# Another hand-written order of units, with other engines for the casts and copies, in a kernel of windowed attention and a maxout layer

## The chip, the core and the metric

The kernel runs on one core of a Trainium2 chip. The metric is device time in microseconds (us), and the median of three runs before the change is 180.03 us (179.86 to 180.07). Engines are called as in the profile: PE is TensorE (PEld its weight loads), DVE VectorE, ACT ScalarE, POOL GpSimd, SP the engine that issues nearly all transfers. A letter q behind an engine means its queue of instructions.

## What is computed

Attention over 4 batches x 8 heads, 768 positions, head size 64, and then a layer in which three products are reduced by a maximum. The mask keeps the first 8 positions (global) and the last 96 before each position (local).

```python
scores = scale * np.matmul(q, k.transpose(0, 1, 3, 2))
keep = is_global | is_local          # pos < 8, or 0 <= rel < 96
bias = -slopes[:, None, None] * dist[None, :, :]
scores = np.where(keep, scores + bias, -1000000000.0)
a = softmax(scores)
x = (a @ v).transpose(0, 2, 1, 3).reshape(3072, 512)
h = np.maximum(np.maximum(x @ w1, x @ w2), x @ w3)   # 512 -> 768
out = h @ w_out                                      # 768 -> 512
```

Inputs and output are float32; the matmuls run in bf16.

## The kernel before

The 3072 positions are 24 tiles of 128, six to a batch. The string `SCHEDULE` is a list of units, and each unit's letter picks a function (the dictionary `units` at the end). Every engine gets its instructions in the order of this list, and so does the SP queue its transfers; nothing reorders them. Numbers behind the letter are the tile or part, and the last one often picks the engine (`copies`: 0 ACT, 1 DVE, 2 POOL).

- Loads, all on SP: `l` (`load_part`, L151, q or k of a group of tiles), `L` (`load`, q and k of one tile), `v` (`load_v`), `w` (`load_w`, w1 to w3: 256 columns for g = 0, 512 for g = 1), `o` (`load_wo`). `raw` has five buffers, `rawv` six.
- Casts to bf16: `c` (`cast_part`), `C` (`cast`: `C T.0` q and k, `C T.1` v; a last number of 3 gives q to DVE and k to POOL), `W`, `Q` (weights).
- Transposes of q and k: `x` (parts; 4 and above split the eviction between ACT and DVE) and `X` (tiles). `X T.4` is a DMA transpose on SP (L250), the others are PE transposes with an eviction.
- Scores `S T.g.how` (`u_S`, L268) for heads 4g to 4g+3, with the exp on ACT (L288). With how = 1 the bias is added by two further matmuls; with 0 the unit `M` multiplies P by a mask on DVE. `K` and `B` make the masks and biases once. `G` (`put_kg`) copies the global keys over the first rows of a tile's k after its own scores, and the next tile's scores need them there. `V` (`put_vg`) does this for v.
- `A T` (`u_A`, L311): P times v on PE, then the normalisation on DVE (L331, L332) into `xb`. `T` (`u_XT`): transposes xb into `xT`, by PE or, with 4, by DMA (L340).
- `F c.f.j` (`u_F1`, L355): one of the 18 products of a chunk (chunks hold 4, 2, 2, 4, 4, 4 and 4 tiles, so matmuls are 512 or 256 wide), evicted by ACT for j = 0 and by a maximum on DVE for j = 1 and 2. `O c.tt.how` (`u_F2`): the second product of one tile, its copy and its store. `E` is the last chunk's second product, with its last store on ACT's queue.
- `D i.n` (`u_D`, L432): n matmuls of zeros that nothing reads.

In PSUM there are three buffers `psH` (F, O, some transposes, D), one `psT` (transposes), and two `sp` tags that scores and `A` share.

Of the kernel before, what the change touches and what calls it, by code (L numbers as in the profile page):

```python
# [22 lines left out]


SCHEDULE = """
    K0 K1 K2 K3 K4 K5 l1.0 l1.1 D0.3 c0.0.2 B0.1 B1.1 B2.1 B3.0 K6 B4.1 B5.1 c0.1.1 c1.0.2 x0.0.4 B6.1
    B7.1 x0.1.4 S0.0.1 v0 l2.0 l2.1 K7 S0.1.1 G0.0 S1.0.1 S1.1.0 x1.0.3 c1.1.2 M0.0 M0.1 M1.0 v1 x1.1.4
    C0.1.2 v2 A0.1 G1.2 S2.0.1 M1.1 c2.0.2 x2.0.1 C1.1.1 S2.1.0 G2.2 S3.0.1 M2.0 M2.1 C2.1.1 T0.1 S3.1.1
    M3.0 M3.1 c2.1.2 v3 A1.0 C3.1.0 w0.0 V1.2 x2.1.2 w1.0 A2.1 V2.2 A3.0 T1.0 T2.1 T3.1 W1.0.1 W0.0.0
    G3.2 S4.0.0 S4.1.0 F0.0.0 F0.1.0 M4.0 F0.2.0 F0.3.0 G4.1 S5.0.0 M4.1 S5.1.0 w0.1 W0.1.1 w0.2 W0.2.2  # L30
    V3.2 F0.0.1 F0.1.1 F0.0.2 F0.1.2 v4 C4.1.0 A4.0 V4.2 w1.1 W1.1.2 W2.0.0 F0.4.0 F0.5.0 M5.0 M5.1 w1.2
    W1.2.2 v5 W2.1.0 T4.0 F0.2.1 F0.3.1 l3.0 l3.2 F0.4.1 l3.1 c3.0.2 c3.2.2 F0.5.1 o2 C5.1.0 A5.1 l3.3
    F0.2.2 Q2.2 F0.3.2 W2.2.0 o0 T5.0 F0.4.2 o1 F0.5.2 x3.0.0 F1.0.0 F1.1.0 c3.1.1 F1.2.0 x3.2.0 Q0.2
    F1.0.1 F1.1.1 F1.2.1 l4.0 l4.1 c3.3.0 F1.0.2 F1.1.2 F1.2.2 x3.1.2 x3.3.1 F1.3.0 F1.4.0 Q1.2 F1.3.1
    S6.0.0 S6.1.0 v6 v7 v8 G6.0 F1.3.2 F1.5.0 v9 c4.0.1 F1.4.1 S7.0.0 S7.1.0 G7.2 v10 M6.0 M6.1 M7.0
    M7.1 O0.0.0 F1.4.2 c4.1.1 C6.1.2 C7.1.2 L12 F1.5.1 S8.0.0 S8.1.0 x4.0.0 O0.1.0 A6.0 x4.1.2 A7.1 V7.2
    F1.5.2 v11 T6.0 O0.2.0 T7.1 G8.2 C8.1.2 S9.0.0 S9.1.0 G9.1 v12 v13 O0.3.0 F2.0.0 F2.1.0 S10.0.0 M8.0
    M8.1 M9.0 M9.1 S10.1.0 C9.1.2 L13 L14 F2.0.1 F2.1.1 F2.0.2 A8.0 C12.0.1 F2.1.2 G10.2 O1.0.0 V8.2
    A9.1 X12.1 M10.0 M10.1 C10.1.0 C11.1.0 F2.2.0 S11.0.0 S11.1.0 M11.0 M11.1 L15 F2.3.0 F2.4.0 O1.1.0
    V9.2 A10.1 F2.2.1 V10.2 T8.0 F2.3.1 F2.5.0 T9.0 A11.1 F2.4.1 T10.0 F2.2.2 F2.3.2 T11.1 F2.4.2  # L40
    S12.0.0 S12.1.0 F2.5.1 C13.0.2 C14.0.2 C15.0.1 X13.4 F3.0.0 F3.1.0 F3.0.1 G12.1 C12.1.0 F3.2.0
    F3.1.1 F3.2.1 S13.0.0 S13.1.0 F2.5.2 v14 C13.1.0 C14.1.2 M12.0 M12.1 F3.0.2 F3.1.2 X14.4 F3.2.2
    X15.4 G13.2 M13.0 M13.1 S14.0.0 S14.1.0 F3.3.0 F3.4.0 F3.5.0 M14.0 M14.1 G14.1 A12.0 A13.1 F3.3.1
    F3.4.1 F3.5.1 S15.0.0 M15.0 S15.1.0 G15.0 v15 V13.2 L16 L17 v16 T12.4 v17 M15.1 O2.0.0 C15.1.0 A14.0
    V14.2 F3.3.2 F3.4.2 T13.4 F3.5.2 C16.1.0 C16.0.2 X16.3 T14.4 C17.0.2 A15.1 X17.4 O2.1.0 S16.0.0
    S16.1.0 G16.1 L18 V15.2 L19 T15.1 M16.0 O3.0.0 M16.1 F4.0.0 F4.1.0 F4.0.1 F4.1.1 C18.0.2 L20 C19.0.2
    A16.1 F4.2.0 F4.3.0 S17.0.0 S17.1.0 F4.2.1 F4.0.2 F4.3.1 v18 M17.0 v19 M17.1 X18.3 X19.4 C20.0.0
    V16.2 F4.1.2 C17.1.2 O3.1.1 A17.1 F4.2.2 F4.3.2 S18.0.0 M18.0 S18.1.0 M18.1 F4.4.0 T16.4 T17.4
    F4.4.1 C18.1.2 C19.1.1 F4.4.2 X20.4 G18.1 S19.0.0 S19.1.0 F4.5.0 L21 M19.0 M19.1 v20 F4.5.1 A18.0
    T18.4 F4.5.2 A19.1 T19.4 V19.1 C21.0.1 X21.4 G19.1 L22 C22.0.2 L23 X22.4 O3.2.1 O3.3.0 O4.0.1  # L50
    S20.0.0 S20.1.0 M20.0 G20.0 O4.1.0 F5.0.0 F5.1.0 F5.2.0 S21.0.0 S21.1.0 G21.2 F5.0.1 F5.1.1 M20.1
    M21.0 F5.3.0 F5.0.2 F5.1.2 F5.2.1 F5.2.2 v21 C20.1.1 C21.1.2 F5.4.0 S22.0.0 M21.1 S22.1.0 C23.0.0
    F5.3.1 M22.0 M22.1 F5.5.0 F5.3.2 A20.0 V20.2 G22.2 v22 F5.4.1 X23.4 v23 F5.5.1 T20.4 A21.1 V21.1
    T21.4 F5.4.2 F5.5.2 S23.0.0 S23.1.0 M23.0 O4.2.0 M23.1 C22.1.2 A22.0 C23.1.0 O4.3.0 V22.2 T22.4
    A23.1 T23.4 O5.0.1 O5.1.0 O5.2.1 O5.3.0 F6.0.0 F6.1.0 F6.0.1 F6.0.2 F6.2.0 F6.3.0 F6.4.0 F6.1.1
    F6.2.1 F6.1.2 F6.3.1 F6.4.1 F6.2.2 F6.3.2 F6.5.0 F6.4.2 F6.5.1 F6.5.2 E
"""


# [1 line left out]
def kernel(  # L61
# [73 lines left out]
    xT = {}  # L135
# [87 lines left out]
    def early(T):  # L223
        return T < NSTART
# [109 lines left out]

    def u_XT(T, how):
        c, i = where[T]
        if i == 0:
            xT[c] = xT_pool.tile([128, NP, len(chunks[c]) * 128], BF16, name="xT", tag="xT")
        if how == 4:
            nc.sync.dma_start_transpose(out=xT[c][:, :, i * 128:(i + 1) * 128],  # L340
                                        in_=xb[T].rearrange("p h d -> p (h d)"))
            return
        if early(T):
            tp = psH.tile([128, NP, 128], BF16, name="xtp", tag="h")
        else:
            tp = psT.tile([128, NP, 128], BF16, name="xtp", tag="tp")
        x = xb[T].rearrange("p h d -> p (h d)")
        for jp in range(NP):
            nc.tensor.transpose(tp[:, jp], x[:, jp * 128:(jp + 1) * 128], identb)  # L349
        copies[how](xT[c][:, :, i * 128:(i + 1) * 128], tp)  # L350

    ht = {}
    h01s = {}

    def u_F1(c, f, j):  # L355
        W = len(chunks[c]) * 128
        if f == 0 and j == 0:
            ht[c] = ht_pool.tile([128, NF, W], BF16, name="ht", tag="ht")
        ps = psH.tile([128, W], FP32, name="h", tag="h")
        for dm in range(4):  # L360
            nc.tensor.matmul(ps, w123[f // 2][:, dm, j, (f % 2) * 128:(f % 2) * 128 + 128],  # L361
                             xT[c][:, dm], start=(dm == 0), stop=(dm == 3))
# [66 lines left out]
    def cast_wo(i, how):  # L429
        copies[how](wo[:, 2 * i:2 * i + 2], wst["o", i])  # L430

    def u_D(i, n):  # L432

        wp = psH.tile([128, 512], FP32, name="wp", tag="h")
        for _ in range(n):
            nc.tensor.matmul(wp, zeros[:, 0:128], zeros, start=True, stop=True)

    with tc.manual_schedule():
# [9 lines left out]
        for tvar in va_ring + va_first:  # L448
# [22 lines left out]

        units = {"l": load_part, "v": load_v, "c": cast_part, "x": u_x, "L": load, "w": load_w, "o": load_wo, "C": cast, "X": u_X, "S": u_S, "M": u_M,
                 "A": u_A, "G": put_kg, "V": put_vg, "T": u_XT, "F": u_F1, "W": cast_w,
                 "K": u_K, "B": u_B, "Q": cast_wo, "O": u_F2, "E": u_E, "D": u_D}
        for u in SCHEDULE.split():
# [34 lines left out]
```

## Time and profile before

| | before |
|---|---|
| median of three runs | 180.03 us |
| profiled execution, span from first to last instruction | 178.3 us |
| granted TensorE clock, mean | 0.997 |
| PE, DVE, ACT, POOL busy | 166.9, 118.9, 103.1, 37.5 us |
| moved by DMA | 35.52 MB, 199 GB/s mean |
| read from and written to HBM | 25.17 MB, 6.29 MB |

Times in the profile count from the first instruction. A row of the timeline is start, length, engine, source line, instruction, tiles (out <- in), shape and count, with the idle time before it and what ended it in brackets. Busy times on PE are modelled, since matmuls overlap; the pace is the start of one to the start of the next. "Chain of waits" is the page's fourth part: the work that ended last, followed back step by step.

### The profile page before, as it was taken

The page shows a single profiled execution, that of the slowest core. Times are in us where ns is not written, and L with a number is a line of the kernel's source. Part 1 is how long each engine was busy: PE and PEld are TensorE (multiplying, and loading weights), DVE is VectorE, ACT ScalarE, POOL GpSimd, SP SyncE. Part 2 cuts the span into 40 slices and gives each one's busy share as a digit, 9 for nine tenths or more (in the row PEclk, how much of TensorE's full clock was granted, in tenths as well). Part 3 has the DMA queues.
Part 4 walks back from the last instruction along what each step waited for, and adds up shares of the span by engine and source line. Part 5 has one row for each costly group of instructions (what it writes and reads, how often), then busy time and mean ns, then how long its engine had stood idle before and what let it go on. Part 6 is the DMA issues. An engine that isn't in the chain of part 4 may idle for free.

```text
span 178.3 us, 3960 instructions
## 1 busy us (share of the span) xinstructions
PE 166.9 (94%) x1529; PEld 95.8 (54%) x1551; DVE 118.9 (67%) x237; ACT 103.1 (58%) x160; POOL 37.5 (21%) x65
## 2 busy tenths in 40 slices
PE   3599799999999999999999999999999999999992
PEld 0455644558867677845555555545444555444442
DVE  4519875986787689748979447979358896136620
ACT  4867898646689858555744837351772643341122
POOL 4355203543343112310007024100020401000000
PEclk9999999999999999999999999999999999999998
DMA  5999999999998999989544999769889674610006
GB/s 140 292 271 242 357 320 384 320 361 358 251 193 213 229 254 236 174 171 233 94 90 118 159 247 235 157 132 186 173 153 294 136 143 146 224 42 4 0 11 226
DMA packets 83587, 35.52 MB, mean 199 GB/s; under 512 B 66160, under 2 KB 78320, under 8 KB 83568
## 3 DMA queue, kind: packets, MB, share of 16 engines
q1 hardware_dynamic: 83424, 35.20, 82.8%
q8 instruction: 12, 0.20, 0.5%
q10 hardware_dynamic: 144, 0.07, 0.1%
q14 instruction: 7, 0.06, 0.1%
HBM read 25.17 MB, written 6.29 MB: 176 GB/s over the span
## 4 chain that ended last, share of the span: by engine, by line
PE 85%; DMA 8%; SPq 2%; issue 1%; POOL 1%; DVE 1%; ACT 1%; ACTq 0%
PE h L361 53%; PE po L376 17%; PE sp L283 6%; DMA rawv<-in_v_dram 4%; DMA rawp<-in_q_dram 4%; PE op L322 3%; PE op L325 2%; SPq L174 2%; PE tpp L239 2%; PE xtp L349 1%; SPq L158 1%; POOL qkp L183 1%; PE tp L261 1%; DVE xb L332 0%; ACT va L189 0%
## 5 line engine op out<-in xcount | busy, mean ns | idle before, releaser
L361 PE MATMUL h<-xT,w 128*128 128x512 bf16 (+1 forms) x491 | 99.2, 348 | 0.7 <-issue 0.2
L361 PEld LDWEIGHTS <-w 128*128 128x128 bf16 x504 | 46.9, 98 | 40.5 <-DVE w L427 0.3
L288 ACT ACTIVATE P<-sp 128x1024 bf16<-128x1024 f32 (+1 forms) x48 | 43.4, 955 | 20.6 <-PE sp L283 20.4
L368 DVE TENSOR_TENSOR h<-h,h 128x512 bf16<-128x512 bf16 (+1 forms) x42 | 25.3, 610 | 25.7 <-PE h L361 16.5
L366 ACT CAST h<-h 128x512 bf16<-128x512 f32 (+1 forms) x42 | 21.6, 533 | 21.5 <-PE h L361 21.3
L376 PE MATMUL po<-wo,ht 128*128 128x512 bf16 (+2 forms) x147 | 33.1, 362 | 0.5
L370 DVE TENSOR_TENSOR ht<-h,h 128x512 bf16<-128x512 bf16 (+1 forms) x42 | 25.1, 607 | 3.7 <-PE h L361 3.0
L307 DVE TENSOR_TENSOR P<-P,wmask 128x1024 bf16<-128x1024 bf16 x36 | 24.8, 718 | 3.6 <-ACT P L288 3.5
L376 PEld LDWEIGHTS <-ht 128*128 128x128 bf16 x156 | 14.0, 98 | 13.9
L382 ACT COPY ost<-po 128x512 f32<-128x512 f32 (+2 forms) x20 | 11.2, 564 | 17.8 <-PE po L376 17.7
L332 DVE TENSOR_TENSOR xb<-op,rz 128x512 bf16<-128x512 f32 x24 | 16.6, 692 | 0.8
L283 PEld LDWEIGHTS <-qkT 64*128 64x128 bf16 x352 | 10.2, 96 | 10.0 <-issue 8.0
L283 PE MATMUL sp<-qkT 64*128 64x128 bf16 x352 | 15.2, 223 | 0.4 <-DVE xb L332 0.4
L322 PEld LDWEIGHTS <-P 128*128 128x128 bf16 x192 | 12.5, 97 | 2.5 <-ACT P L288 0.2
L221 POOL COPY va<-vaf 8x260 int32<-8x260 int32 x14 | 6.3, 452 | 34.5 <-PE op L325 34.5
L198 POOL CAST qkb<-raw 128x1024 bf16<-128x1024 f32 x7 | 7.2, 1037 | 27.7 <-DMA raw<-in_q_dram 18.9
L322 PE MATMUL op<-va,P 128*128 128x65 bf16 x160 | 12.3, 193 | 0.7 <-ACT va L189 0.6
L239 PE MATMUL tpp<-identb,qkp 128*128 128x128 bf16 x96 | 8.5, 246 | 4.0 <-POOL qkp L183 3.4
L325 PEld LDWEIGHTS <-P 128*128 128x128 bf16 x160 | 10.4, 97 | 2.2 <-issue 0.7
L239 PEld LDWEIGHTS <-qkp 128*128 128x128 bf16 x96 | 7.0, 111 | 5.8 <-POOL qkp L183 4.3
L325 PE MATMUL op<-va,P 128*128 128x65 bf16 x128 | 9.9, 193 | 0.0
L243 ACT COPY qkT<-tpp 128x1024 bf16<-128x1024 bf16 (+1 forms) x9 | 7.9, 874 | 3.4 <-PE tpp L239 3.4
(66 smaller groups left out, 107.5 us busy)
## 6 DMA issues: line engine op xcount, KB each, us to landing
rawv<-in_v_dram SPq DMA_DIRECT2D x24, 256.0 KB, 4.8
out_dram<-ost SPq DMA_DIRECT2D x23, 256.0 KB, 2.3
rawp<-in_q_dram SPq DMA_DIRECT2D x6, 512.0 KB, 7.2
rawp<-in_k_dram SPq DMA_DIRECT2D x6, 512.0 KB, 7.4
wst<-in_moe_w_dram SPq DMA_DIRECT2D x3, 1024.0 KB, 9.7
raw<-in_q_dram SPq DMA_DIRECT2D x12, 256.0 KB, 4.1
raw<-in_k_dram SPq DMA_DIRECT2D x12, 256.0 KB, 4.8
wst<-in_moe_w_dram SPq DMA_DIRECT2D x3, 512.0 KB, 8.7
```

Of the source, the lines that this page charges most:

```text
L239: nc.tensor.transpose(tp[:, e, j - lo], qb["p", n, s][:, e, 2 * j:2 * j + 2].rearrange("i h d -> i (h d)"), identb)
L283: nc.tensor.matmul(sp[:, hh, j2, ds], qT(T - ds, 1)[hsl, jp], qT(T, 0)[hsl, jp], start=not how, stop=True, skip_group_check=True)
L288: nc.scalar.activation(P[:, :, 0:n], sp.rearrange("p a b d n -> p (a b) d n")[:, :, 0:n], AF.Exp, bias=0.0, scale=scale)
L307: nc.vector.tensor_mul(P, P, wmask[:, g, :, 0:2])
L322: nc.tensor.matmul(o, P[:, i, 0], heads(va[T])[:, h], start=True, stop=(t == 0), skip_group_check=True)
L325: nc.tensor.matmul(o, P[:, i, 1], heads(va[T - 1])[:, h], start=False, stop=True, skip_group_check=True)
L332: nc.vector.tensor_tensor(out=x.rearrange("p (g h) d -> p g h d", g=2), in0=o4[:, :, :, 0:64], in1=rz[:, :, :, None].to_broadcast([128, 2, ...
L361: nc.tensor.matmul(ps, w123[f // 2][:, dm, j, (f % 2) * 128:(f % 2) * 128 + 128], xT[c][:, dm], start=(dm == 0), stop=(dm == 3))
L366: nc.scalar.copy(h01, ps)
L368: nc.vector.tensor_max(h01s[c, f], h01s[c, f], ps)
L370: nc.vector.tensor_max(ht[c][:, f], h01s[c, f], ps)
L376: nc.tensor.matmul(po, ht[c][:, f, tt * 128:(tt + 1) * 128], wo[:, f, cols], start=(f == 0), stop=(f == NF - 1))
```

## The change

In a few words it is described as: units queued in another order with casts of v and copies of global values on GpSimd; of q, k and weights only the first two groups' casts there. The whole list is written anew, and three functions change a little: `xT[c]` and `ht[c]` are now made by whichever unit of a chunk comes first, and `D` may stand with no count. The source lines move down by 2 to 4. The functions that a unit calls are the same.

```diff
 SCHEDULE = """
-    K0 K1 K2 K3 K4 K5 l1.0 l1.1 D0.3 c0.0.2 B0.1 B1.1 B2.1 B3.0 K6 B4.1 B5.1 c0.1.1 c1.0.2 x0.0.4 B6.1
-    B7.1 x0.1.4 S0.0.1 v0 l2.0 l2.1 K7 S0.1.1 G0.0 S1.0.1 S1.1.0 x1.0.3 c1.1.2 M0.0 M0.1 M1.0 v1 x1.1.4
-    C0.1.2 v2 A0.1 G1.2 S2.0.1 M1.1 c2.0.2 x2.0.1 C1.1.1 S2.1.0 G2.2 S3.0.1 M2.0 M2.1 C2.1.1 T0.1 S3.1.1
-    M3.0 M3.1 c2.1.2 v3 A1.0 C3.1.0 w0.0 V1.2 x2.1.2 w1.0 A2.1 V2.2 A3.0 T1.0 T2.1 T3.1 W1.0.1 W0.0.0
-    G3.2 S4.0.0 S4.1.0 F0.0.0 F0.1.0 M4.0 F0.2.0 F0.3.0 G4.1 S5.0.0 M4.1 S5.1.0 w0.1 W0.1.1 w0.2 W0.2.2
...
-    A23.1 T23.4 O5.0.1 O5.1.0 O5.2.1 O5.3.0 F6.0.0 F6.1.0 F6.0.1 F6.0.2 F6.2.0 F6.3.0 F6.4.0 F6.1.1
-    F6.2.1 F6.1.2 F6.3.1 F6.4.1 F6.2.2 F6.3.2 F6.5.0 F6.4.2 F6.5.1 F6.5.2 E
+    K6 K5 D1.2 D4.8 B2.1 B4.1 B7.1 B5.1 l1.0 l1.1 K4 B6.1 v0 B1.0 B3.1 c0.0.1 K1 K3 x0.0.2 K7 B0.1
+    c0.1.1 x0.1.4 G0.2 c1.0.1 c1.1.1 K0 S0.0.1 S1.1.1 M1.1 S1.0.0 G1.2 x1.0.3 S0.1.1 x1.1.0 K2 M0.0
+    C0.1.1 M0.1 A0.1 v1 C1.1.2 S2.0.0 M1.0 S2.1.0 G2.1 T0.1 M2.0 S3.0.0 S3.1.1 M3.1 v2 l2.0 c2.0.1
+    M2.1 M3.0 C2.1.2 v3 A1.0 x2.0.2 V1.2 G3.2 A2.1 C3.1.2 T1.0 V2.2 l2.1 c2.1.1 A3.0 V3.0 w0.0 T2.0
+    w0.1 x2.1.4 T3.1 W0.0.0 S4.0.0 W0.1.1 S4.1.0 w0.2 D3.1 F0.0.0 G4.1 M4.1 M4.0 F0.1.0 F0.1.1
+    W0.2.0 F0.0.1 S5.1.0 w1.0 W1.0.0 W2.0.1 S5.0.0 F0.1.2 v4 C4.1.1 F0.0.2 M5.1 F0.4.0 w1.1 A4.1
...
+    F1.4.0 F1.1.0 F1.0.0 l3.3 c3.3.0 o0 Q0.0 x3.1.3 F0.4.2 F1.0.1 x3.3.0 F1.2.0 G6.0 F1.2.1 F1.1.1
+    l4.1 o1 S6.0.0 S6.1.0 v6 C6.1.2 Q1.1 F1.0.2 F1.5.0 F1.5.1 S7.0.0 S7.1.0 G7.1 F1.4.1 F1.5.2
+    c4.1.1 F1.3.0 o2 Q2.0 F1.4.2 M7.1 v7 S8.0.0 M6.1 l4.0 c4.0.0 L12 L14 C7.1.2 v9 v8 L13 M7.0
+    S8.1.0 F1.1.2 v11 O0.3.1 v13 v10 M6.0 A7.0 G8.2 F1.3.1 C12.0.0 O0.0.0 v12 x4.1.2 T7.1 A6.0
...
+    T8.4 T9.4 F2.4.0 F2.5.1 C14.0.1 X14.4 v15 F2.4.1 S11.0.0 S11.1.0 O1.1.0 M11.0 M10.1 M10.0 F2.2.1
...
+    F6.1.1 F6.0.0 F6.4.0 F6.0.1 F6.4.1 F6.4.2 F6.5.0 F6.5.1 F6.1.2 F6.2.0 F6.2.1 F6.0.2 F6.2.2
+    F6.3.1 F6.3.2 F6.5.2 E D2.8 D0.3
 """
...
-        if i == 0:
+        if c not in xT:
...
-        if f == 0 and j == 0:
+        if c not in ht:
...
-    def u_D(i, n):
+    def u_D(i, n=0):
+        if n == 0:
+            return
```

Counted over both whole lists, by the engine that the last number picks:

| units | before: ACT, DVE, POOL | after: ACT, DVE, POOL |
|---|---|---|
| `c`, casts of q/k parts | 1, 4, 7 | 4, 8, 0 |
| `C T.0`, casts of q/k tiles | 2, 3, 7 | 6, 4, 0, and 2 split between DVE and POOL |
| `W` and `Q`, casts of weights | 4, 2, 6 | 7, 5, 0 |
| `C T.1`, casts of v | 10, 4, 10 | 6, 2, 16 |
| `V`, copies of global values | 0, 2, 14 | 5, 5, 6 |
| `G`, copies of global keys | 4, 7, 9 | 7, 3, 10 |
| `O`, copies of results | 15, 5, 0 | 10, 10, 0 |

DMA transposes are 9 `X` and 11 `T` before, 10 and 13 after. Scores with a bias matmul are 6 before and 4 after. The zero matmuls are 3 before and 22 after: ten at the start, one before F0.0.0, and eleven behind `E`.

More of the change, by code (lines that the diff above doesn't have):

```diff
@@ L31 @@
[L31 to L54, printed above, removed]
-    A23.1 T23.4 O5.0.1 O5.1.0 O5.2.1 O5.3.0 F6.0.0 F6.1.0 F6.0.1 F6.0.2 F6.2.0 F6.3.0 F6.4.0 F6.1.1
@@ new lines @@
+    W0.2.0 F0.0.1 S5.1.0 w1.0 W1.0.0 W2.0.1 S5.0.0 F0.1.2 v4 C4.1.1 F0.0.2 M5.1 F0.4.0 w1.1 A4.1
+    V4.1 W1.1.1 W2.1.1 w1.2 v5 F0.3.0 M5.0 F0.5.0 F0.2.0 F0.2.1 T4.1 F0.3.1 F0.4.1 W1.2.0 F0.2.2
+    C5.1.2 A5.1 W2.2.0 F0.3.2 l3.0 F0.5.1 c3.0.0 T5.1 l3.2 c3.2.0 F0.5.2 x3.2.2 l3.1 c3.1.1 x3.0.1
+    F1.4.0 F1.1.0 F1.0.0 l3.3 c3.3.0 o0 Q0.0 x3.1.3 F0.4.2 F1.0.1 x3.3.0 F1.2.0 G6.0 F1.2.1 F1.1.1
+    l4.1 o1 S6.0.0 S6.1.0 v6 C6.1.2 Q1.1 F1.0.2 F1.5.0 F1.5.1 S7.0.0 S7.1.0 G7.1 F1.4.1 F1.5.2
+    c4.1.1 F1.3.0 o2 Q2.0 F1.4.2 M7.1 v7 S8.0.0 M6.1 l4.0 c4.0.0 L12 L14 C7.1.2 v9 v8 L13 M7.0
@@ new lines @@
+    S8.1.0 F1.1.2 v11 O0.3.1 v13 v10 M6.0 A7.0 G8.2 F1.3.1 C12.0.0 O0.0.0 v12 x4.1.2 T7.1 A6.0
+    O0.1.1 S9.1.0 S9.0.0 V7.1 M8.0 T6.0 x4.0.3 F1.2.2 M8.1 O0.2.1 M9.0 M9.1 C8.1.0 F2.5.0 F2.0.0
+    G9.2 S10.0.0 S10.1.0 G10.2 F1.3.2 C9.1.2 F2.0.1 F2.0.2 A8.0 X12.0 F2.2.0 C13.0.3 V8.2 A9.1 X13.4
+    T8.4 T9.4 F2.4.0 F2.5.1 C14.0.1 X14.4 v15 F2.4.1 S11.0.0 S11.1.0 O1.1.0 M11.0 M10.1 M10.0 F2.2.1
+    S12.0.0 S12.1.0 F2.2.2 M11.1 F2.5.2 V9.2 C10.1.2 A10.0 V10.1 C11.1.2 L15 O1.0.0 F2.1.0 F2.4.2
+    C13.1.2 A11.0 T10.0 F2.1.1 F2.3.0 S13.1.0 G12.0 S13.0.0 L18 T11.1 M12.1 F2.3.1 F2.3.2 M12.0
@@ new lines @@
+    G13.2 C15.1.2 L16 v14 C14.1.2 F3.5.0 F3.4.0 F3.4.1 F2.1.2 C12.1.0 M13.1 S14.0.0 M14.0 C15.0.0
+    X15.4 S14.1.0 F3.5.1 M13.0 F3.1.0 A12.0 M14.1 F3.4.2 F3.2.0 F3.0.0 A13.0 V13.0 F3.1.1 C16.0.0
+    G14.0 F3.2.1 F3.2.2 L19 F3.3.0 C18.0.0 X16.0 L17 F3.1.2 S15.1.0 S15.0.0 C19.0.1 T12.4 G15.0
+    F3.3.1 F3.0.1 F3.0.2 X18.4 T13.4 C17.0.0 A14.1 F3.3.2 V14.1 F3.5.2 M15.0 X19.4 S16.0.0 L20 T14.4
+    S16.1.0 M16.1 v18 C18.1.2 v17 v16 O2.0.0 X17.4 O3.2.0 S18.0.0 v19 S18.1.0 G16.0 O3.3.0 M15.1
+    A15.0 V15.0 O3.1.0 C20.0.1 M18.1 X20.4 T15.0 M18.0 O3.0.0 F4.3.0 A18.0 M16.0 F4.2.0 F4.0.0
@@ new lines @@
+    S19.1.0 M19.1 C16.1.0 S19.0.0 L21 F4.0.1 F4.3.1 L22 A16.1 C19.1.0 L23 T16.4 F4.3.2 F4.2.1 G18.0
+    V16.0 M19.0 F4.2.2 T18.4 S17.0.0 S17.1.0 F4.1.0 F4.5.0 F4.5.1 G19.2 M17.1 F4.1.1 A19.1 F4.1.2
+    M17.0 F4.4.0 C17.1.2 F4.4.1 C21.0.3 F4.4.2 S20.0.0 S20.1.0 C22.0.1 F4.0.2 T19.4 F4.5.2 v20 X21.4
+    A17.0 T17.4 O4.0.0 C23.0.0 X22.4 v21 O4.3.1 v22 V19.1 G20.0 O4.2.1 v23 O4.1.1 S21.0.0 S21.1.0
+    F5.2.0 F5.1.0 M20.0 M21.0 M20.1 F5.1.1 C20.1.2 F5.5.0 F5.1.2 A20.1 M21.1 G21.2 F5.0.0 F5.2.1
+    S22.0.0 V20.0 S22.1.0 G22.2 F5.5.1 F5.5.2 F5.0.1 F5.4.0 M22.0 C21.1.0 X23.4 S23.1.0 M23.1
@@ L57 @@
+    S23.0.0 F5.4.1 F5.4.2 A21.1 T21.4 V21.2 C22.1.2 M23.0 T20.4 O2.1.0 M22.1 F5.3.0 F5.3.1 C23.1.0
+    F5.0.2 A22.0 T22.4 F5.2.2 F5.3.2 V22.2 A23.0 T23.4 O5.3.1 O5.0.1 O5.2.1 O5.1.1 F6.3.0 F6.1.0
+    F6.1.1 F6.0.0 F6.4.0 F6.0.1 F6.4.1 F6.4.2 F6.5.0 F6.5.1 F6.1.2 F6.2.0 F6.2.1 F6.0.2 F6.2.2
+    F6.3.1 F6.3.2 F6.5.2 E D2.8 D0.3
 """
```

## The prediction

> **What bounds the kernel now.** I read the page first, then the busy time by stretch, then the chain of waits, and only then single rows.
>
> ```profile
> span 178.3 us, 3960 instructions
> ...
> PE 166.9 (94%) x1529; PEld 95.8 (54%) x1551; DVE 118.9 (67%) x237; ACT 103.1 (58%) x160; POOL 37.5 (21%) x65
> ...
> PE   3599799999999999999999999999999999999992
> ...
> DMA  5999999999998999989544999769889674610006
> ...
> PE 85%; DMA 8%; SPq 2%; issue 1%; POOL 1%; DVE 1%; ACT 1%; ACTq 0%
> ```
>
> PE is full from the sixth slice to the last, and it makes up 85% of the chain that ended last. The 16 DMA engines are full too for the first half. The stretch rows (start and end, length, then busy time of PE, PEld, DVE, ACT and POOL, the granted clock, DMA share and GB/s) split the run at 23.44, where the first matmul of the second layer stands:
>
> ```profile
> 23.44:175.10 151.66, 150.32 (x1324) 85.39 (x1344) 104.23 (x196) 85.72 (x132) 28.09 (x42) 1.00 0.81 190
> ```
>
> From there to 175.10 PE is idle for only 1.34 us in all. So three numbers make the time: when the F work starts, how much PE work follows, and what hangs behind it. The chain of waits gives what sets the start, and the pace of each kind of PE work (start, length, what, count):
>
> ```profile
> 13.07 7.08 DMA rawv<-in_v_dram
> 20.18 0.63 ACT va L189
> ...
> 22.52 0.40 PE xtp L349 x4
> 22.92 0.55 PE sp L283 x16
> 23.48 0.34 PE h L361
> ...
> 33.60 3.45 PE h L361 x16
> ...
> 46.04 0.89 PE tpp L239 x16
> 46.94 1.31 PE h L361 x12
> ...
> 50.58 0.36 POOL qkT L216
> ...
> 119.61 0.26 PE op L322 x8
> ```
>
> The start is set by v of tile 3: it lands at 20.18, is cast, and A3, T3 and S4 follow, then F0.0.0 at 23.48. The paces are 3.45/16 = 0.216 us for a 512-wide matmul, 1.31/12 = 0.109 for 256, 0.89/16 = 0.056 for a transpose, 0.034 for a score and 0.033 for a P·v matmul. Behind F0.0.0 stand, by the unit list, 360 + 144 wide F1 matmuls (93.5 us), 144 for F2 (31.1), 280 scores (9.6), 296 P·v (9.6), 72 q/k transposes and 36 of x (6.0): 149.8 us of the 151.6. There is next to nothing to win inside; less work on PE or an earlier start is what pays.
>
> **The words and the diff.** The words tell of global values copied on GpSimd and of casts of the first two groups left there. Counted in the unit list, the copies V on GpSimd fall from 14 to 6 of 16, casts of v there rise from 10 to 16 of 24, and of the q, k and weight casts 20 whole ones leave GpSimd and two half ones (tiles 13 and 21) come. I go by the list.
>
> **The front.** Rows of the timeline (start, length, engine, instruction, idle before):
>
> ```profile
> 1.19 1.46 PE L436 MATMUL wp<-zeros 128*128 128x512 bf16 x3 [1.19 <-DVE tiny L443]
> ...
> 4.95 1.07 POOL L183 CAST qkp<-rawp 128x1024 bf16<-128x1024 f32 x1 [1.86 <-DMA rawp<-in_q_dram]
> 6.08 1.03 PE L239 MATMUL tpp<-identb,qkp 128*128 128x128 bf16 x8 [3.43 <-POOL qkp L183]
> ...
> 6.73 0.69 DVE L183 CAST qkp<-rawp 128x1024 bf16<-128x1024 f32 x1 [1.60 <-DMA rawp<-in_k_dram]
> ...
> 12.20 1.69 PE L239 MATMUL tpp<-identb,qkp 128*128 128x128 bf16 x16
> ...
> 22.24 1.05 ACT L427 CAST w<-wst 128x1024 bf16<-128x1024 f32 x1
> ```
>
> The first q cast moves to DVE behind six bias tiles. Those end near 5.5, and the cast (0.69) near 6.2 instead of 6.02: 0.2 later. Ten zero matmuls in place of three run 10 x 1.46/3 = 4.9 us, from 1.19 to 6.1, so they end as the cast does and delay nothing; they cost something only if the cast came sooner. The first 16 transposes ran at 0.13 each, 16 later ones at 0.106, the warm ones at 0.056. The pace doubled only after PE had worked with gaps for some 7 us, and the zeros now supply most of that. Sixteen transposes at 0.056 save about 1.1 us of PE time, half of it on the path.
>
> The Trainium skill (TensorE: Matmul & The Clock Gate, "What's actually happening") says that the array starts at half clock and is released by about 3.4 us of sustained work. By that rule the first transposes run at full pace and the start comes 0.4 us earlier; with the cold pace kept it would come 0.4 later, 0.8 us on the sum. The trace's pace agrees with it, though its granted clock reads 1.00 throughout.
>
> Next the queue. v of tiles 1 and 2 now go out ahead of q of group 2, and v of tile 3 ahead of its k; ten transfers precede the first weight as before. So the weight that F0.0.0 needs lands no sooner:
>
> ```profile
> 14.98 4.33 SPq L417 DMA_DIRECT2D wst<-in_moe_w_dram  x4
> ...
> wst<-in_moe_w_dram SPq DMA_DIRECT2D x1, 512.0 KB, 6.7
> ```
>
> That is 14.98 + 6.7 = 21.7; with the 1.05 cast F0.0.0 can start at 22.75 at best. ACT is the brake, since it does this cast after it has evicted its half of x2.1. The tenth transfer, v of tile 3, landed at 20.18; now k of group 2 is the tenth. Its cast on DVE (0.69) ends at 20.9, its transposes (0.45) at 21.4, ACT's half of the eviction (some 0.6) at 22.0, the weight cast at 23.1. If DVE is still busy with the normalisations of tiles 1 and 2 (0.9 each, 0.7 of it overlapping), it is 23.9. I take 23.1, as the v of tile 3 is off the chain: **-0.4 us** (bounds -0.7 and +0.4). Two score units lose their bias matmuls (4 x 0.216 = 0.9 us of PE), but they stand before the start, where PE waits anyway, and DVE gets two masks more.
>
> **Work moved off PE.** Behind the start one tile's q/k and two tiles' x change from PE transposes to DMA transposes: 8 + 8 transposes at 0.056, **-0.9 us**. They land in time if there is room:
>
> ```profile
> xT<-xb SPq DMA_TRANSPOSE x11, 2.4
> qkT<-qkb SPq DMA_TRANSPOSE x9, 3.2
> ```
>
> T8 and T9 are queued right behind their tiles, with 10 us of PE work ahead of F3.5.0, which needs them; 2.4 us and a queue of some eight transfers fit. Without that room F3 would wait 2 to 3 us. The one extra zero matmul before F0.0.0 costs 0.2 inside the front's bounds. The other changes of order, and eight copies V that go to ACT and DVE, take no PE time and stay under its 1.3 us of slack or F work.
>
> **Casts moved from GpSimd.** Their prices (line, engine, form, count, busy us, mean ns):
>
> ```profile
> L198 POOL CAST qkb<-raw 128x1024 bf16<-128x1024 f32 x7 | 7.2, 1037 | 27.7 <-DMA raw<-in_q_dram 18.9 <-DMA raw<-in_k_dram 8.8
> L198 ACT CAST qkb<-raw 128x1024 bf16<-128x1024 f32 x2 | 2.1, 1052 | 0.1
> L198 DVE CAST qkb<-raw 128x1024 bf16<-128x1024 f32 x3 | 2.0, 681 | 0.0
> L288 ACT ACTIVATE P<-sp 128x1024 bf16<-128x1024 f32 x40 | 39.0, 1027 | 15.4 <-PE sp L283 15.2
> L307 DVE TENSOR_TENSOR P<-P,wmask 128x1024 bf16<-128x1024 bf16 x36 | 24.8, 718 | 3.6 <-ACT P L288 3.5
> ```
>
> Twenty whole casts at 1.04 leave POOL (-20.8 us). ACT takes ten of them (+10.5) and loses four v casts and five output copies; DVE takes eight more and the two halves (some +6.5), five output copies and two masks (some +5 at 0.68 to 0.72). So DVE goes to about 130 of 178 us and ACT to 109: neither becomes the bound on average. One stretch is close. From F1.2.0 to O0.0.0 the new list gives ACT 3 narrow evictions, 6 exps, 3 casts, a copy and an output, 10.4 us, against 9.7 us of PE. Before, the same stage read:
>
> ```profile
> 35.00:40.00 5.00, 4.95 (x41) 2.67 (x41) 4.13 (x8) 2.37 (x4) 2.28 (x3) 1.00 1.08 359
> 43.00:57.00 14.00, 13.95 (x180) 11.03 (x179) 10.54 (x22) 11.77 (x19) 4.69 (x7) 1.00 0.99 231
> ```
>
> ACT was busy 84% there and PE lost nothing. Consecutive ACT instructions overlap (two exps of 1.03 take 1.95):
>
> ```profile
> 27.58 1.95 ACT L288 ACTIVATE P<-sp 128x1024 bf16<-128x1024 f32 x2
> ```
>
> So 10.4 becomes 9.9 and the excess is 0.2. The other cost is standing: a cast that waits for its data on POOL stops nobody, and on ACT it stops the evictions and exps queued behind it, for which PE then waits with three psH buffers. Below, it is nothing, as every cast comes after its landing; above, it is the rival's price. I take **+0.4** for both. The stall on GpSimd's key copy (0.36 at 50.58) goes, as S8 now stands 1.7 us of F work behind it; what is late next is exp S8, so I count no gain.
>
> **The end.**
>
> ```profile
> 174.30 0.72 PE L376 MATMUL po<-wo,ht 128*128 128x128 bf16 x10
> ...
> 175.10 0.27 ACT L382 COPY ost<-po 128x128 f32<-128x128 f32 x1 [0.30 <-PE po L376]
> 175.40 0.37 ACTq L383 DMA_DIRECT2D out_dram<-ost  x1
> ...
> out_dram<-ost ACTq DMA_DIRECT2D x1, 64.0 KB, 1.9
> ```
>
> Eleven zero matmuls now follow the last real one: 11 x 0.216 = 2.4 us from 175.02, so to 177.4, while the last store lands at 175.40 + 1.9 = 177.3. The store covers all but **+0.1**; without that cover it would be 2.4.
>
> **Sum.** 178.3 - 0.4 - 0.9 + 0.4 + 0.1 = 177.5 for the span. The median of the runs, 180.03, stands 1.7 us above the profiled span, so 179.2; I forecast 179.3.
>
> **The rivals.**
> *ACT stands before data (slower).* The place is c4.0.0 and C12.0.0 on ACT. PE reaches S8.1 26.5 us of work after F0.0.0, near 49.9; two exps and c4.0.0 make it 53 when ACT comes to C12.0.0. Its data are 5.24 MB behind the first part of group 3, which landed at 36.8:
>
> ```profile
> 36.77 1.04 POOL L183 CAST qkp<-rawp 128x1024 bf16<-128x1024 f32 x1 [1.58 <-DMA rawp<-in_q_dram]
> ```
>
> At 359 GB/s they land at 51.4, at 231 at 59.5; three fifths come in long rows, so 54 is likelier. From about 55 on every us is lost, as O0.0.0's copy and the exps of S9 wait behind it. With a mean of 2.5 us lost here, and at L15 and L19 later, the time is 181.8. For it: 18.9 us of POOL's standing shows how far data can lag. Against it: the loads are queued earlier too.
> *The gain doubles.* The start comes at 22.75 and the remaining 1.3 us of PE's idle time go with the looser order: 177.8. For it: my count finds no long wait. Against it: idle time of that kind came with every order that the trace shows.
> *Nothing.* ACT holds the start at 23.9 and eats the transposes' 0.9: 180.0. The words not being what the list does changes no price.
>
> **The numbers.** Forecast 0.40 (own range 178.4 to 179.8), slower 0.31, nothing 0.16, double gain 0.13. A measurement of this kernel tells 0.2%, 0.36 us, from no change. Faster takes the forecast but for its top and the double gain: 0.51; same 0.18; slower 0.31. The range 177.6 to 182.0 leaves out the ends of the outer cases.
>
> **What would show it.** First transposes in about 0.5 us and F0.0.0 at 22.75 to 23.9; PE idle behind it under 2 us; T rows at thirteen DMA transposes landing before F3 and F5; ACT's waits for DMA near nothing; the last store, and not PE, ending the run. An ACT wait of over 1 us for raw or rawp, followed by PE waiting for an eviction, makes it wrong; so does a start after 24.

## The result and the profile after

| | before | after |
|---|---|---|
| median | 180.05 us (179.86 to 180.07, 4 runs) | 179.02 us (178.85 to 179.17, 4 runs) |
| span of the profiled execution | 178.3 us | 177.4 us |
| granted TensorE clock, mean | 0.997 | 0.99 |

The ratio is 0.9942, 95% interval 0.993 to 0.9953: faster by 1.0 us. The forecast was 179.3, with 177.5 for the span. (Ratios here and below are of mean times and leave out runs over 1.5% above the fastest of their kernel, medians are of all runs; left out are three runs of e11 and the profiled one of e8, span 184.6 against 181.7 to 182.3 in its other four, from which only the order of events is read below.)

The page of after, its head, the granted clock in 40 slices, and the shares of the chain that ended last:

```profile
span 177.4 us, 3967 instructions
...
PE 170.6 (96%) x1550; PEld 95.7 (54%) x1550; DVE 126.5 (71%) x248; ACT 109.7 (62%) x166; POOL 19.9 (11%) x46
...
PEclk9879999999999999999999999999999999999999
...
PE 90%; DMA 3%; issue 2%; ACT 2%; DVE 2%; SPq 0%; POOL 0%
```

The chain now holds 3% of DMA where it held 8%: the transfer of v of tile 3 is gone from it. ACT is busy as long as forecast (109.7 us against 109), DVE a little less (126.5 against 130), and POOL has half its work left.

The front in the timeline of PE (the zeros, two tiles' transposes, F0.0.0), then on ACT the cast of the first weight:

```profile
1.19 3.69 PE L440 MATMUL wp<-zeros 128*128 128x512 bf16 x10 [1.19 <-DVE tiny L447]
6.06 0.62 PE L241 MATMUL tpp<-identb,qkp 128*128 128x128 bf16 x8 [1.19 <-DVE qkp L185]
7.49 1.04 PE L241 MATMUL tpp<-identb,qkp 128*128 128x128 bf16 x8 [0.81 <-DVE qkp L185]
...
23.06 3.63 PE L363 MATMUL h<-xT,w 128*128 128x512 bf16 x16
```

```profile
21.95 1.05 ACT L429 CAST w<-wst 128x1024 bf16<-128x1024 f32 x1
```

F0.0.0 starts at 23.06; before, the row of the second layer's first matmuls started at 23.44. The cast of its weight ends at 23.00, and the chain of waits arrives there at the same moment by another way, through DVE:

```profile
19.69 0.69 DVE xb L334
20.38 0.60 DVE qkp L185
...
21.13 0.70 DVE xb L334
...
21.88 0.40 PE xtp L351 x4
22.27 0.60 PE sp L285 x16
22.87 0.32 PE wp L440
```

Two normalisations (xb) with the cast of k of group 2 (qkp) between them, back to back: in this execution the start is set by work on DVE and by ACT's cast, not by a transfer.

That is not so in every execution. e2 below has the same list up to its end, and there the chain comes from the transfer of k of group 2, which DVE waits for:

```profile
12.49 7.73 DMA rawp<-in_k_dram
...
20.25 0.69 DVE qkp L185
```

Issued within 0.1 us of each other, k landed at 20.2 in e2 and near 18.7 in after (12.45 + 6.3). e3 and e5 are like e2 (19.8 and 20.1). F0.0.0 started at 23.02 in e2, 22.63 in e3 and 22.86 in e5: both paths end within 0.4 us of each other.

Behind the start, the stretch of F0.0.0 to the last real matmul (columns as in the prediction), and the group of all F1 matmuls (count, busy us, mean ns, idle before):

```profile
23.06:174.10 151.04, 151.03 (x1330) 84.59 (x1330) 109.61 (x203) 90.71 (x137) 13.98 (x26) 1.00 0.85 195
```

```profile
L363 PE MATMUL h<-xT,w 128*128 128x512 bf16 (+1 forms) x504 | 100.6, 349 | 0.0
```

The stretch of before was 151.66; by the ends of the last real matmuls (175.02 before, 172.82 + 1.27 = 174.09 after, shown below) it went from 151.58 to 151.03, 0.55 less. The F1 matmuls show no idle time. Pauses show only in the pace, and in one place of the chain:

```profile
49.84 0.33 PE sp L285 x8
...
50.18 0.40 PE sp L285 x8
...
52.42 0.18 PE op L324
```

Sixteen scores take 0.60 at 22.27 and, to the end of the second eight, 0.74 here (S8.1 stood a little); A7's first matmul takes 0.18 where the others take 0.03. Set against e11 below, whose units are the same up to here, the two come to 0.34 us, in the very stretch that the prediction called close.

The end of the timeline:

```profile
172.82 1.27 PE L378 MATMUL po<-wo,ht 128*128 128x256 bf16 x16
...
173.93 2.54 PE L440 MATMUL wp<-zeros 128*128 128x512 bf16 x11
...
174.42 0.37 ACTq L385 DMA_DIRECT2D out_dram<-ost  x1
```

The zeros end at 176.47, the span at 177.4: the last store ends the run, 2.98 after its issue (before: 178.3 - 175.40 = 2.9).

So the 0.9 us of the span: 0.38 at the start, 0.55 behind it (0.90 of transposes less, some 0.35 of pauses more), nothing at the end.

### The profile page after: what moved, and what is told of

Same layout as the page of the kernel before. It is cut to its first block, busy times and chain, and to the rows that moved or that the text cites. A ratio compares the mean times of both kernels' runs of the same rounds, so it can differ in the third digit from the quotient of the medians.

```text
span 177.4 us, 3967 instructions
## 1 busy us (share of the span) xinstructions
PE 170.6 (96%) x1550; PEld 95.7 (54%) x1550; DVE 126.5 (71%) x248; ACT 109.7 (62%) x166; POOL 19.9 (11%) x46
## 4 chain that ended last, share of the span: by engine, by line
PE 90%; DMA 3%; issue 2%; ACT 2%; DVE 2%; SPq 0%; POOL 0%
PE h L363 54%; PE po L378 18%; PE sp L285 7%; DMA rawp<-in_k_dram 3%; PE op L324 3%; PE op L327 2%; PE tpp L241 2%; PE wp L440 2%; ACT P L290 1%; PE xtp L351 1%; PE sp L277 1%; DVE xb L334 1%; DVE qkp L185 1%; ACT qkT L245 1%; PE tp L263 1%
## 5 line engine op out<-in xcount | busy, mean ns | idle before, releaser
L363 PE MATMUL h<-xT,w 128*128 128x512 bf16 (+1 forms) x504 | 100.6, 349 | 0.0
L290 ACT ACTIVATE P<-sp 128x1024 bf16<-128x1024 f32 (+1 forms) x48 | 43.9, 956 | 12.3 <-PE sp L285 12.1
L309 DVE TENSOR_TENSOR P<-P,wmask 128x1024 bf16<-128x1024 bf16 x38 | 25.4, 686 | 6.1 <-ACT P L290 5.8
L384 ACT COPY ost<-po 128x512 f32<-128x512 f32 (+2 forms) x15 | 8.2, 555 | 14.5 <-PE po L378 14.4
L324 PEld LDWEIGHTS <-P 128*128 128x128 bf16 x192 | 12.5, 97 | 3.6 <-DVE ht L372 0.5
L191 POOL CAST va<-rawv 128x512 bf16<-128x512 f32 x14 | 9.6, 692 | 41.0 <-DMA rawv<-in_v_dram 16.5
L384 DVE COPY ost<-po 128x512 f32<-128x512 f32 (+1 forms) x11 | 7.2, 653 | 9.2 <-PE po L378 9.1
L324 PE MATMUL op<-va,P 128*128 128x65 bf16 x160 | 12.5, 193 | 0.1
L241 PE MATMUL tpp<-identb,qkp 128*128 128x128 bf16 x96 | 7.6, 227 | 2.2 <-DVE qkp L185 2.2
L245 ACT COPY qkT<-tpp 128x1024 bf16<-128x1024 bf16 (+1 forms) x8 | 7.3, 916 | 2.0 <-PE tpp L241 2.0
L241 PEld LDWEIGHTS <-qkp 128*128 128x128 bf16 x96 | 6.1, 101 | 3.8 <-DVE qkp L185 3.0
```

The source lines that it names most:

```text
L241: nc.tensor.transpose(tp[:, e, j - lo], qb["p", n, s][:, e, 2 * j:2 * j + 2].rearrange("i h d -> i (h d)"), identb)
L290: nc.scalar.activation(P[:, :, 0:n], sp.rearrange("p a b d n -> p (a b) d n")[:, :, 0:n], AF.Exp, bias=0.0, scale=scale)
L309: nc.vector.tensor_mul(P, P, wmask[:, g, :, 0:2])
L324: nc.tensor.matmul(o, P[:, i, 0], heads(va[T])[:, h], start=True, stop=(t == 0), skip_group_check=True)
```

## Experiments: the front

**e1**: three zero matmuls at the start, as before the change.

```diff
-    K6 K5 D1.2 D4.8 B2.1
+    K6 K5 D1.3 B2.1
```

> The new order with three zero matmuls at the start, as before, in place of ten. Theory (the front is set by the chain of casts, evictions and exps, and a warm first group of transposes is not waited for, since k of the group lands at 6.72): time 179.0, the same within 0.2, F0.0.0 still near 23.1, first 8 transposes back at about 1.03 us. Rival (the warm array is what brought the start forward): 179.4 to 179.8, F0.0.0 at 23.5 or later.

179.54 us median of 12, ratio 0.9986 (0.9967 to 1.0005). Eight runs lie at 179.02 to 179.70 and four at 180.63 to 180.78; the profiled one is of the four. Its timeline (lines one lower, as the list is shorter):

```profile
6.06 1.03 PE L240 MATMUL tpp<-identb,qkp 128*128 128x128 bf16 x8 [3.41 <-DVE qkp L184]
...
11.35 1.04 PE L240 MATMUL tpp<-identb,qkp 128*128 128x128 bf16 x8
```

The transposes at 6.06 take 1.03 instead of 0.62, those of the third tile still 1.04, and both stand on this profile's chain of waits. F0.0.0 starts at 24.99 here; why so late is told in the last section. No profile of the commoner runs was kept, but their times lie where the rival had them: the zeros are worth 0.5 us in them.

**e12**: the other way round, ten zeros in the kernel before.

```diff
-    K0 K1 K2 K3 K4 K5 l1.0 l1.1 D0.3 c0.0.2
+    K0 K1 K2 K3 K4 K5 l1.0 l1.1 D1.2 D4.8 c0.0.2
```

> The kernel before with ten zero matmuls at the start in place of three, nothing else. Theory (in the old order v of tile 3, which lands at 20.18, sets the start, so that a warm array only waits longer): F0.0.0 at 23.4 to 23.5, 180.0. Rival (the warm array alone brings the start forward, by the 0.4 us of the forecast): F0.0.0 at 23.1, 179.6. The zeros end at about 6.1 while the first q cast on GpSimd ends at 6.02, so 0.1 us of delay is in both.

180.11 us median of 12, ratio 1.0018 (0.9997 to 1.0039). Ten runs lie at 179.81 to 180.29 and two at 181.7 and 181.8. The theory holds for the ten: in the old order a warm array gains nothing, as v of tile 3 comes when it comes. It is on the chain of the profiled run too, which is one of the two long ones (F0.0.0 at 24.20).

**e7**: the old order of transfers, group 2 ahead of v of tiles 1 to 3.

```diff
-    l2.0 and l2.1 behind v2 and v3
+    l2.0 l2.1 v1
```

> The changed kernel with both loads of group 2 (q and k) moved ahead of v of tiles 1, 2 and 3, which is the order of transfers before. Theory (the start came forward because v of tile 3 left the chain): v3 lands last, about 19, the chain runs through its cast, A3 and T3 again, F0.0.0 at 23.5 or later, 179.3 to 179.6. Rival (the order of these loads is worth nothing, and the start hangs on the first weight at 21.3 and its cast by ACT): F0.0.0 at 23.1, 179.0.

180.6 us median of 12 (lowest 180.01), ratio 1.0043 (1.0022 to 1.0063). The chain of waits:

```profile
13.07 7.01 DMA rawv<-in_v_dram
...
20.70 0.41 POOL va L223
...
22.41 0.70 DVE xb L334
...
24.52 0.39 PE h L363
```

The transfer of v is back on the chain, with the copy of the global values behind it, and the start goes to 24.5. Part of that is PE's pace, for the granted clock reads 0.50 from 15.5 to 22 in this profile. The price is free of it in the two runs with a granted clock of 1.00: 180.40 and 180.45, 1.4 us above the changed kernel's two at that clock (179.08 and 178.96). So the theory's direction holds, and the price is more than the whole gain of the front. That everything else stands ready earlier in the new order and waits for this tile would explain it, but is not shown.

**e6**: c0.0 and the casts of groups 1 and 2 on GpSimd, close to what the words of the change say (c0.1 stays on DVE).

```diff
-    c0.0.1 c1.0.1 c1.1.1 c2.0.1 c2.1.1
+    c0.0.2 c1.0.2 c1.1.2 c2.0.2 c2.1.2
```

> The changed kernel with c0.0, c1.0, c1.1, c2.0 and c2.1 on GpSimd, as the words of the change say, and not on DVE. Theory (DVE holds the start: c2.1 is cast 1.66 us after its data landed at 18.72, behind normalisations): c2.1 starts at 18.8 and ends at 19.9 instead of 20.98, F0.0.0 some 0.3 to 0.5 us earlier, 178.6. Rival (what counts in the front is the length of the first casts, 0.69 on DVE against 1.04 on GpSimd, and the copies of global values that stand behind them there): F0.0.0 at the same time or up to 1 us later, 179.0 to 180.0.

180.17 us median of 12, ratio 1.0007 (0.9996 to 1.0019); span 177.7. POOL's timeline:

```profile
19.47 0.61 POOL L191 CAST va<-rawv 128x512 bf16<-128x512 f32 x1
20.13 0.39 POOL L223 COPY va<-vaf 8x260 int32<-8x260 int32 x1
20.48 1.03 POOL L185 CAST qkp<-rawp 128x1024 bf16<-128x1024 f32 x1
```

The rival holds: the cast of c2.1 stands behind a v cast and a copy and starts at 20.48, no sooner than on DVE (20.38), and then takes 1.03 instead of 0.60; F0.0.0 starts at 23.61. The times lie 2.1 to 2.2 us above their spans in this kernel and 1.7 to 1.8 in the changed one; what these 0.4 us outside the span are stays open.

**e2**: without the eleven zeros at the end.

```diff
-    F6.5.2 E D2.8 D0.3
+    F6.5.2 E
```

> The new order without the eleven zero matmuls behind E. Theory (they end 0.15 us after the last store lands, and the end takes as long as before): 178.9 to 179.0, at most 0.15 us faster. Rival (they hold the end back by their 2.4 us): 176.7.

179.06 us median of 6 (178.79 to 179.90), ratio 0.9952 (0.9934 to 0.997), span 177.3. The zeros are free behind the store, and removing them gains nothing.

## Experiments: the transposes

**e4**: the three additional DMA transposes in the kernel before, at the places of the PE ones.

```diff
-    T8.0 T9.0 X18.3
+    T8.4 T9.4 X18.4
```

> The old order with T8, T9 and X18 alone turned into DMA transposes. Theory (PE work is the bound): 0.9 us faster than before, 179.1 to 179.2, so most of the change's gain without its order. Rival (the old order has no room on the transfer queue, so F3 or S18 waits): 180.0 or more, with PE waiting for xT or qkT.

180.34 us median of 11, ratio 1.0011 (1.0002 to 1.0019). On PE and on SP's queue:

```profile
76.35 5.34 PE L363 MATMUL h<-xT,w 128*128 128x512 bf16 x24 [1.02 <-DMA xT<-xb]
```

```profile
70.92 2.79 SPq L342 DMA_TRANSPOSE xT<-xb  x2
```

Both went out between 70.92 and 73.71, and F3.0.0, due at 75.3, waited for them 1.02 us: the rival holds, and the 0.9 us gain is eaten by one wait. In the changed kernel they go out 4 us sooner, against an F3.5.0 that is due at 74.72 + 8 x 0.109 = 75.6:

```profile
66.52 2.55 SPq L342 DMA_TRANSPOSE xT<-xb  x2
```

**e10**: the same three, with T8 behind V8 and T9 behind V9 in the old list.

```diff
-    V8.2 ... V9.2 ... T8.0 ... T9.0
+    V8.2 T8.4 ... V9.2 T9.4
```

> The kernel before with the same three transposes by DMA, T8 right behind V8 and T9 right behind V9 in the list, as early as the old order allows. Theory (what the old order lacked was room between T8, T9 and the F3 product that reads them): F3 no longer waits, -0.9, 179.2. Rival (SP's queue, not the list, decides when these transposes go out, or something else holds them): still about 180.3 with PE waiting for xT near 75.

180.62 us median of 6, ratio 1.0036 (1.0024 to 1.0047). On PE, on DVE (the xb of tile 9), and on SP:

```profile
76.30 5.35 PE L363 MATMUL h<-xT,w 128*128 128x512 bf16 x23 [1.50 <-DMA xT<-xb]
```

```profile
66.02 0.69 DVE L334 TENSOR_TENSOR xb<-op,rz 128x512 bf16<-128x512 f32 x1
```

```profile
70.34 0.95 SPq L385 DMA_DIRECT2D out_dram<-ost  x1
71.39 1.23 SPq L342 DMA_TRANSPOSE xT<-xb  x1
```

T9's source was ready at 66.71, but T9 stood in SP's queue behind two loads and the store of O1.1, went out at 71.39, and PE had it at 76.30, 4.9 us later. The rival holds: the queue decides, and the place that I called the earliest was not. A place ahead of that store wasn't tried, so whether the old order could have had the gain stays open.

**e3** and **e9**: the changed kernel with the three transposes on PE again, T8 and T9 next to each other, and apart.

```diff
-    T8.4 T9.4 F2.4.0 F2.5.1 C14.0.1 X14.4 v15 F2.4.1 ... F2.2.1 ... X18.4
+e3  F2.4.0 F2.5.1 C14.0.1 X14.4 v15 F2.4.1 T8.0 T9.0 ... F2.2.1 ... X18.0
+e9  F2.4.0 F2.5.1 C14.0.1 X14.4 v15 F2.4.1 T8.0 ... F2.2.1 T9.0 ... X18.0
```

> The new order with T8, T9 and X18 on PE again (16 transposes and three evictions on ACT). Theory (PE work behind the start is the bound): 16 x 0.056 = 0.9 us slower, 179.9. Rival (order and engines made the gain, transposes are hidden): 179.0.

> The changed kernel with T8, T9 and X18 on PE again, T8 and T9 apart (behind F2.4.1 and F2.2.1), so that the single psT buffer is free for each. Theory (16 transposes on PE cost 0.056 us each and nothing else): +0.9, 179.9. Rival (they cost more than their pace, by the copies that ACT and DVE get with them in a full stretch, or less, as PE has pauses to fill): 180.4 or more, or 179.0 to 179.4.

e3: 180.83 us median of 6, ratio 1.0054 (1.0038 to 1.007). It is no clean undo, since T9 waits for ACT's copy of T8 out of the one psT buffer:

```profile
66.31 0.38 PE L351 MATMUL xtp<-identb,xb 128*128 128x128 bf16 x4 [0.67 <-ACT xT L352]
```

e9, without that wait: 180.07 us median of 12, ratio 1.0014 (0.9997 to 1.0031), nine of them at 179.69 to 180.18. Its profile starts F0.0.0 at 23.06, as after, and its span is 178.4: the whole 1.0 us lies behind the start, so the 0.9 us of the sum is right. The other three, at 181.09 to 181.15, are taken up in the last section.

**e8** and **e11**: more of them. e8 puts X12, T10 and X16 on the DMA, the first two early; e11 only X16, at its old place.

```diff
+e8  C12.0.0 X12.4 ... V10.1 T10.4 ... X16.4   (X12.0 and T10.0 gone)
+e11 X16.4
```

> The changed kernel with three more transposes by DMA: q/k of tiles 12 and 16 and x of tile 10, issued early. Theory (each PE transpose taken away behind the start is 0.056 us of PE, as long as the DMA lands ahead of its reader): 8 + 8 + 4 = 20 transposes, -1.1 us, 177.9. Rival (the room is used up: the added transposes or those behind them on SP's queue land after their readers are due, and PE waits as it did when the kernel before was given three of them): 178.8 to 180.5, with a wait of PE for xT or qkT in the trace.

> The changed kernel with one more transpose of q/k by DMA, that of tile 16, at its old place: 7 us of PE work stand between it and the scores that read it (87.79 to 94.66), against about 4 us from issue to landing. Theory (with room each transpose taken off PE is worth its 0.056 us): -0.45, 178.6. Rival (it pushes T12, T13, T14 and X18 back by 1.3 us in SP's queue and one of them then comes too late): 179.0 or more, with PE waiting for xT or qkT between 95 and 104.

e8: 183.95 us median of 5, ratio 1.0215 (1.0202 to 1.0228). On SP and on PE:

```profile
61.02 4.30 SPq L252 DMA_TRANSPOSE qkT<-qkb  x1
...
69.51 3.29 SPq L342 DMA_TRANSPOSE xT<-xb  x2
...
76.67 1.23 SPq L342 DMA_TRANSPOSE xT<-xb  x1
```

```profile
79.94 0.58 PE L363 MATMUL h<-xT,w 128*128 128x512 bf16 x1 [4.15 <-issue]
```

X12 holds SP's queue for 4.30 us, T8 and T9 go out 3 us later than after, T10 at 76.67 when its reader is due, and F3 stands 4.15 us. The view names no releaser ("issue"); that it is T10 follows from the order alone. The rival holds.

e11: ratio 0.9952 (0.993 to 0.9973); median 179.52 of 12 runs from 178.45 to 181.50. Its profile is the shortest of all: F0.0.0 at 22.95, span 176.5, 0.9 less than after. Of that 0.11 is the start, and set against after matmul by matmul the two pauses near 50 and 52 are gone (0.34) and 0.44 is gained at the place of X16, near 89, as the theory has it. But the runs spread so widely, with a granted clock of 1.00 too (178.62 and 178.71, 180.05 and 180.35), that the times don't show a gain over the changed kernel (0.9942). No version here is measurably faster than it.

## Experiment: the casts

**e5**: all casts of q and k from group 3 on, and of w_out, on GpSimd, as most of them were.

```diff
-    c3.*.0/1 c4.*.0/1 C12.0.* to C23.0.* Q*.0/1
+    c3.*.2   c4.*.2   C12.0.2 to C23.0.2 Q*.2
```

> The changed kernel with all casts of q and k from group 3 on (c3, c4, C12.0 to C23.0) and of w_out (Q) back on GpSimd, the order kept. Theory (the stalls of 0.20 us at 49.95 and 0.15 us at 52.04 come from ACT and DVE having too much in that stretch, so the +0.4 of the forecast is real): both stalls go, PE idle behind F0.0.0 falls by 0.2 to 0.35 us, time 178.7. Rival (the casts cost nothing where they are; on GpSimd they are 0.35 us longer each and stand before data in its queue, with the v casts and G copies behind them): no gain, 179.0, or up to 1 us slower where a G copy or a DMA transpose comes too late.

181.87 us median of 6, ratio 1.0103 (1.0078 to 1.0128). The pause of S8.1 went, as it did in e2 and e11 with the casts where they were, so that shows nothing. The waits of PE in this run are (engine and line, waited for; us, times, longest):

```profile
PE op L324 <- POOL va L191: 1.2, 1, 1.2
PE op L324 <- POOL vaf L191: 0.8, 1, 0.8
```

And POOL's timeline at the first of them:

```profile
51.28 1.35 POOL L185 CAST qkp<-rawp 128x1024 bf16<-128x1024 f32 x1 [1.02 <-DMA rawp<-in_q_dram]
52.59 0.61 POOL L191 CAST va<-rawv 128x512 bf16<-128x512 f32 x1
```

The cast c4.0.0 stands 1.02 us before its data on POOL and takes 1.35, and behind it stands the cast of v for A7, for which PE waits. The theory falls. The rival's mechanism holds, but not its price of at most 1 us: on GpSimd these casts cost 2.8 us more. In the profile the span is 2.3 us longer, and the two waits add up to 2.0.

## Why the prediction was right

**The front, -0.4.** Measured -0.38, for the reason given: v of tile 3 left the chain (e7). The prediction had k of group 2 land last, be cast by 20.9 and go through DVE, PE and ACT. In e2 it is so (cast by 20.94); in the profile of after it lands earlier and waits for DVE between two normalisations, which stood only among the bounds. ACT's weight cast ended at 23.00, against 23.1 forecast.

**The zeros.** The first transposes took 0.62, against about 0.5 forecast and 1.03 before. The ten zeros took 3.69 us and not 4.9, for the prediction priced all ten at the pace of the first three; they cost no time either way. The Trainium skill (TensorE: Matmul & The Clock Gate, "What's actually happening") has the array run at full pace after some 3.4 us of sustained work; the transposes behind 3.69 us of zeros agree. It has the array fall back after an idle window of the same length. The trace shows otherwise: the second tile's transposes ran at 1.04 after pauses of 1.19 and 0.81 us, and the stretches show the clock down (granted clock third from the end):

```profile
5.00:8.00 3.00, 1.13 (x13) 0.96 (x14) 1.97 (x5) 2.63 (x6) 0.00 (x0) 0.90 1.22 290
8.00:11.00 3.00, 3.00 (x29) 1.46 (x27) 1.88 (x3) 1.91 (x5) 0.52 (x1) 0.53 1.27 260
```

It cost little: e2, e3 and e5, in whose front the clock stays up, started at 22.63 to 23.02 instead of 23.06. That the warm array gains by itself is half true: 0.5 us in the new order (e1), none in the old (e12).

**The transposes, -0.9.** Right, with room as the condition (e9, e4, e8).

**The casts, +0.4.** The term that was mis-sized. The pauses of 0.35 us are there in the profile of after, but not in those of e2, e7 and e11, which have the same casts there, so 0 to 0.35 is the size, and that the span came out within 0.1 of the 177.5 is partly luck. What makes these pauses stays open. And the step held that a cast that waits for its data on POOL stops nobody; in e5 it stops the v casts behind it, and PE with them. The new order lives on POOL being free.

The stall of 0.36 at 50.58, which was to go, was none. In the kernel before, O0.0.0 and the next products stand on PE like this:

```profile
50.48 1.47 PE L376 MATMUL po<-wo,ht 128*128 128x512 bf16 x5
51.78 1.04 PE L361 MATMUL h<-xT,w 128*128 128x256 bf16 x8
```

O0.0.0 has six matmuls, and from 50.48 to 51.78 are 1.30 us, six at 0.216: PE did not stand, a record is missing (see the last section).

**ACT before data**, the slower rival, didn't come, by little. The prediction had ACT come to C12.0.0 at 53 and its data at 54. The two casts on ACT, and of the transfers issued between 43 and 50 the first part of group 4 and the k of tile 12 (the last number is the us from issue to landing; issued at 43.05 and 47.95):

```profile
52.12 1.07 ACT L185 CAST qkp<-rawp 128x1024 bf16<-128x1024 f32 x1
...
53.97 1.08 ACT L200 CAST qkb<-raw 128x1024 bf16<-128x1024 f32 x1
```

```profile
rawp<-in_q_dram SPq DMA_DIRECT2D x1, 512.0 KB, 8.1
...
raw<-in_k_dram SPq DMA_DIRECT2D x1, 256.0 KB, 5.4
```

Landings at 51.15 and 53.35: ACT came 1.0 and 0.6 us behind its data. In the whole run it waits for transfers twice, 0.5 us each, both at casts of q and k parts. **Nothing** and **the doubled gain** fell with the sum.

**The end, +0.1.** Nothing: the store ended the run, as before (e2).

## What to carry to other kernels

Price a cast by what stands behind it in its engine's queue, not by its length alone: casts that cost 0.35 us at most on ACT and DVE cost 2.8 where they stood before their data in GpSimd's queue. A DMA transpose frees PE only if its source is ready, and SP's queue free, some 5 us ahead of the reader; otherwise one wait gives the gain back (e4, e10). And the parts of a rewritten order aren't a sum: taken out of the new list, the zeros, the loads, the casts and the transposes each cost 0.5 to 2.8 us, while two of them put into the old one gained nothing.

## What had not been expected of the hardware

The times of one and the same kernel come in groups, and the granted clock tells most of them apart (runs by their mean granted clock, times in us):

| kernel | shorter runs | longer runs |
|---|---|---|
| e1 | 8, clock 1.00: 179.02 to 179.70 | 4, clock 0.99: 180.63 to 180.78 |
| e9 | 9, clock 0.99 to 1.00: 179.69 to 180.18 | 3, clock 0.981: 181.09 to 181.15 |
| e2 | 4, clock 0.99 to 1.00: 178.79 to 179.14 | 2, clock 0.981: 179.80 and 179.90 |
| e12 | 10, clock 0.99 to 1.00: 179.81 to 180.29 | 2, clock 0.98 and 0.991: 181.80 and 181.70 |

The traces show what stands behind the mean. In steps of half a microsecond the granted clock reads 0.50 from 7.5 to 10.5 in after, far ahead of F0.0.0, where it cost little: the changed kernel ran 179.17 and 178.85 with a mean of 0.99, 179.08 and 178.96 with 1.00. In the profile of e1, one of its long runs, it reads 0.50 from 17.5 to 20.5, when P times v of tile 1 and the transposes behind it are on the chain, and F0.0.0 starts at 24.99. In that of e12, also a long one, it does so from 9.5 to 12.5 and again from 23.0 to 26.0, over F0.0.0 itself. In that of e9, a shorter run, it does so from 15.5 to 18.5, and F0.0.0 still starts at 23.06. By these traces the same loss of clock is nearly free or costs over a microsecond, by where it falls. The kernel before was within 179.65 and 180.34 in all 30 runs beside the last experiments, with 0.996 to 1.00. None of the changed kernel's four runs was long, but two of e2's six were, and its list differs only behind `E`. What starts such a stretch stays open.

Not every idle time on PE is one. The same six matmuls of the second product, O0.3's, in after and in e11:

```profile
50.96 1.46 PE L378 MATMUL po<-wo,ht 128*128 128x512 bf16 x6
```

```profile
50.67 1.46 PE L378 MATMUL po<-wo,ht 128*128 128x512 bf16 x5
```

Five take the 1.46 us of six: a record is missing, and a pause of 0.22, one matmul, appears in the pace where there was none. The prediction's 1.34 us of idle time behind the start are partly of this kind, for its stretch holds 1324 records, and that of after 1330 with sixteen transposes fewer.
